# An attention and expert-layer kernel on one Trainium2 core: score buffers, PSUM banks and the turning of tiles redistributed

## The chip, the core and the metric

The kernel runs on one core of a Trainium2 chip. A core has TensorE (PE in the profile; PEld is its loading of weights), VectorE (DVE), ScalarE (ACT), GpSimd (POOL) and SyncE (SP), which here issues all DMAs. They work in parallel, each in its own fixed order, and wait for each other by semaphores. Working memory is SBUF; TensorE writes its results to PSUM, which has eight banks of 512 fp32 columns in each of 128 partitions, and the others read them there. The metric is the time of one execution on the device, in microseconds (us), lower being better.

## The reference

Sparse attention, then two gated feed-forward layers over all tokens:

```
scores = scale * q @ k.T;  thresh = max(scores) - tau          # 4 batches, 8 heads, 576 x 576, head 64
scores = where(scores >= thresh, scores, -1e9)
attn = exp(scores - max(scores));  attn /= sum(attn) + 1e-9
x = attn @ v                                                    # as 2304 tokens x 512
x = x / rms(x) * rms_g
x = (silu(x @ w_gate) * (x @ w_val)) @ w_out                    # 512 -> 1536 -> 512
x = (silu(x @ w_gate2) * (x @ w_val2)) @ w_out2
```

tau is 0.02 here. With a negative one no score of a row would pass, and the reference would give all 576 keys the same weight; the kernel takes care of that case too.

## The kernel before

`body` doesn't issue instructions straight away. Each operation is entered with `op` (L77) in a `Program` with its engine, an estimated cost in ns, the keys that it reads and writes, its buffers and a priority `p` (a due time). `order` (L104) then plays a list schedule with these costs and emits the instructions in the order that it finds. On the chip every engine keeps that order, whatever the true durations are.

**Attention.** A batch has 36 tiles (`NTB`): 4 pairs of heads, 9 tiles of 128 query rows for each pair. `tile_ops` (L368) makes one tile: scores into two PSUM banks (`QK`, L388); the row maximum (L398); from it threshold and bias by `K1`, two constants in spare columns of the score bank (L399); the exponential (L400); the mask, which also sums the row (L401). For the product with the values the masked tile has to be turned. `by_pe` (L206) decides how: on TensorE (five transposes L420, copies out L423, fp32 values L431, output L434), which holds for 24 tiles of batch 0 and 18 of batch 1; or it is split into two fp16 parts (high L441 or L444, low L442 on GpSimd or L445 on VectorE), turned by a DMA transposition (L448), and multiplied with the values in three bf16 parts (L464); one output sums the parts (L469 for two tiles in batches 2 and 3, L472 for one). `finish` (L476) handles a group of nine tiles: rows in which nothing passes get the mean of the values (`v_mean`, L353), and all are scaled by the reciprocal, in six GpSimd operations (L494 to L502). `rms` (L504) normalises a batch and writes it, turned and in two parts, to `XS`, what the dense layers read.

**Dense layers.** Phases in the order of `PHASES` (L186), (batch, layer): (0,0), (1,0), (0,1), (1,1), (2,0), (2,1), (3,0), (3,1). They are called phases 0 to 7 here. A phase has 18 weight units and 36 groups of 12 matmuls (`dense`, L626; matmuls L636), each group in a PSUM bank of its own; the last batch has more columns and two banks for a group. The groups are emptied by L662 and L663 (gate), L666 (value), L691 and L693 (output); L670 and L671 split the hidden part. Weights come as fp64: in phases 0 and 2 each unit is converted (L582 on ScalarE, L585 to L588 on VectorE) and split into two parts (L590, L592: VectorE for the first layer, GpSimd for the second), and kept in device memory for the later phases.

**What sets the order.** `DS` and `DD` (L188) are due times and lengths of the phases, `SPAN` (L199) those of a batch's tiles; `FP` is the planned time of a tile of batch 0. Phase 0 needs all of batch 0, phase 1 all of batch 1, phase 4 batch 2, phase 6 batch 3.

**PSUM.** `SA` (two banks) holds scores; `DA` and `DB` (two each) hold four dense banks, and in batch 0 serve as second score buffer (`DA`) and for transposed tiles (`DB`); two banks `PT` take turns for values and normalisation. From batch 1 on all scores use `SA`, and the fifth transposed piece of a tile goes to its spare columns (L413).

Of the kernel before, what the change touches and what calls it, by code (L numbers as in the profile page):

```python
# [69 lines left out]
class Program:  # L70


    def __init__(self):
        self.eng, self.cost, self.deps, self.fn, self.prio, self.lat, self.name, self.cols, self.rel = [], [], [], [], [], [], [], [], []
        self.wrote, self.read = {}, {}

    def op(self, eng, cost, fn, r=(), w=(), bufs=(), p=0.0, lat=None, name='', cols=None, rel=0.0):  # L77
# [26 lines left out]
    def order(self):  # L104
# [19 lines left out]
        out, seen = [], {}  # L124
        while len(out) < n:
# [46 lines left out]

@with_exitstack
def body(ctx: ExitStack, tc: tile.TileContext, qkv, tau, w1, rg, w2, outT):
# [24 lines left out]
    SPAN = [(A0, A0 + NTB * FP), (DS[0] + 1000, DS[1] - 14000), (DS[1], mid), (mid, DS[6] - 16000)]  # L199
# [21 lines left out]
    ones = sb.tile([P, P], F32, name="ones")  # L221
    nc.gpsimd.memset(ones, 1.0)
# [8 lines left out]
    K1 = SA[:, 0, 508:510]  # L231
# [64 lines left out]
    op("ACT", 200, lambda: nc.scalar.copy(K1, K0), w=["K1"], p=0, name="K1")  # L296
    op("DMA", 625, lambda: nc.sync.dma_start(rgs, rg), w=["rg"], p=9000, name="rg")

    def spread_g():
# [29 lines left out]
    def split_v(hd):  # L329
# [15 lines left out]
        parts = [v.t[:, :, 64 * i:64 * i + 64] for i in range(3)]  # L345
# [3 lines left out]
        for i, x in enumerate((V, R)):  # L349
            op("POOL", 500, lambda i=i, x=x: nc.gpsimd.tensor_scalar(parts[i], x, 1.0, 1.0, ALU.mult, ALU.mult), r=[("rawv", hd)], **k)  # L350
            op("POOL", 800, lambda i=i, x=x: nc.gpsimd.tensor_tensor(R if i == 0 else parts[2], x, parts[i], ALU.subtract), r=[("rawv", hd)], **k)

    def v_mean(g):  # L353

        p = ST(g * NT) + 5 * FP
        pt, pk = next_pt()
        vs = vsum[g]
        vb = r_vb.next()
        op("PE", 400, lambda: nc.tensor.matmul(pt[:, :P], ones, vs.t.rearrange("p h d -> p (h d)"), start=True, stop=True), r=[("vs", 2 * g), ("vs", 2 * g + 1)], w=pk, bufs=[vs], p=p, name=f"vsum{g}")
        for o, i in ((vb.t[:, :P], pt[:, :P]), (vb.t[0:64, P:], pt[0:64, 0:64]), (vb.t[64:, P:], pt[64:, 64:P])):  # L360
            op("ACT", 200, lambda o=o, i=i: nc.scalar.activation(o, i, AF.Copy, scale=UPP), w=pk + [("vb", g)], bufs=[vb], p=p, name=f"vsum{g}")
# [430 lines left out]
```

## Time and profile before

| | |
|---|---|
| Median of 3 runs | 1427.27 us (1425.29 to 1430.33) |
| The profiled execution | 1425.47 us |
| Its span, first to last instruction | 1423.7 us |
| Mean granted TensorE clock | 0.923 of 2.4 GHz |
| PE, DVE, ACT, POOL busy | 1285.2, 781.2, 480.0, 463.0 us |

Times in the rows further down count from the start of the span. A "busy" TensorE is one with a matmul under way; it is not one at its peak. A row of windows gives for one stretch its length, the busy time of each engine with its number of instructions, the mean granted clock (1.00 is 2.4 GHz, 0.50 is 1.2 GHz), the mean busy share of the DMA engines and what they moved. In a group of instructions, "busy" is followed by the mean length of one in ns, then the idle time of its engine just before them and what ended it.

### The profile page before, as it was taken

How to read it: one execution, taken by the hardware profiler on the slowest of the kernel's cores; microseconds unless marked ns; L12 is line 12 of the kernel's file. 1: busy time of each engine (PE TensorE's matmuls, PEld its weight loads, DVE VectorE, ACT ScalarE, POOL GpSimd, SP SyncE). 2: the span in 40 equal slices, each digit the busy share in tenths (PEclk: the TensorE clock that was granted, in tenths of full speed). 3: DMA queues.
4: the chain of work that ended last, by engine and by line, in shares of the span. 5: the costliest groups of instructions: out<-in, count | busy, mean ns of one | idle time of the engine just before them, and what ended most of it. 6: DMA issues, size and time to landing. Idle time of an engine off the chain costs nothing.

```text
span 1423.7 us, 18094 instructions
## 1 busy us (share of the span) xinstructions
PE 1285.2 (90%) x6946; PEld 1024.9 (72%) x6946; DVE 781.2 (55%) x1282; ACT 480.0 (34%) x785; POOL 463.0 (33%) x532
## 2 busy tenths in 40 slices
PE   7988799987659998878899999999999999999998
PEld 5656576664437766655677777677777899999998
DVE  5676699894482448979954655455554311222122
ACT  5653455443341324443333423323332221122110
POOL 5644325252141236563632324132211211132111
PEclk9955699995569999989999999999999999999999
DMA  5366176784255666678796577676666333333332
GB/s 167 85 180 180 42 250 215 249 267 126 58 119 168 191 185 217 203 242 279 226 272 190 176 220 215 182 198 185 185 185 185 130 137 118 121 139 126 119 125 97
DMA packets 178870, 247.47 MB, mean 174 GB/s; under 512 B 141408, under 2 KB 149600, under 8 KB 155744
## 3 DMA queue, kind: packets, MB, share of 16 engines
q1 hardware_dynamic: 178784, 246.32, 56.7%
q8 instruction: 54, 0.88, 0.3%
q14 instruction: 32, 0.26, 0.0%
HBM read 170.40 MB, written 42.47 MB: 150 GB/s over the span
## 4 chain that ended last, share of the span: by engine, by line
PE 72%; DVE 14%; issue 4%; ACT 3%; DMA 3%; POOL 3%; SPq 0%; ACTq 0%; POOLq 0%; DVEq 0%
PE ps L636 57%; PE ps L388 5%; PE pt L464 4%; PE pt L431 3%; DMA U<-U 3%; DVE th L666 2%; DVE col L398 2%; PE ps L420 2%; DVE U L401 1%; DVE U L445 1%; ACT U L400 1%; DVE w L586 1%; DVE Y L693 1%; DVE w L587 1%; DVE w L588 1%
## 5 line engine op out<-in xcount | busy, mean ns | idle before, releaser
L636 PE MATMUL ps<-FU,w 128*128 128x512 f32 (+1 forms) x2592 | 619.3, 391 | 47.2 <-DVE th L666 21.4
L636 PEld LDWEIGHTS ps<-FU,w 128*128 128x128 f32 x2592 | 474.5, 191 | 159.8 <-issue 29.2
L636 PE MATMUL ps<-XS,w 128*128 128x384 f32 (+1 forms) x1728 | 348.4, 359 | 6.0 <-DVE th L666 3.9
L636 PEld LDWEIGHTS ps<-XS,w 128*128 128x128 f32 x1728 | 308.4, 190 | 37.6 <-DVE th L666 10.1
L671 POOL TENSOR_TENSOR FU<-th,FU 128x512 fp32r<-128x512 f32 x72 | 103.7, 1441 | 352.2 <-ACT FU L670 352.2
L400 ACT ACTIVATE U<-ps,col 128x576 f32<-128x576 f32 x144 | 106.5, 741 | 175.1 <-DVE col L399 170.6
L401 DVE SCALAR_TENSOR_TENSOR U<-ps,col,U 128x576 f32<-128x576 f32 x144 | 116.9, 813 | 64.9 <-ACT U L400 64.7
L388 PE MATMUL ps<-U 64*128 64x288 f32 (+1 forms) x640 | 129.4, 527 | 23.4 <-DVE U L401 17.5
L398 DVE TENSOR_REDUCE col<-ps 128x1 f32<-128x576 f32 x144 | 108.3, 752 | 72.4 <-PE ps L388 53.5
L671 POOL TENSOR_TENSOR FU<-U,FU 128x768 fp32r<-128x768 f32 x24 | 44.0, 1834 | 234.8 <-ACT FU L670 234.8
L464 PEld LDWEIGHTS <-U 128*128 128x128 f16 (+1 forms) x1120 | 79.6, 107 | 42.7 <-issue 26.9
L464 PE MATMUL pt<-U,U 128*128 128x192 bf16 (+3 forms) x1120 | 98.4, 249 | 6.6 <-DMA U<-U 6.2
L445 DVE SCALAR_TENSOR_TENSOR U<-U 128x576 f16<-128x576 f32 x90 | 87.5, 972 | 21.3 <-ACT U L444 20.8
L663 DVE SCALAR_TENSOR_TENSOR U<-U,ps 128x768 f32<-128x768 f32 x24 | 22.9, 954 | 134.9 <-ACT U L662 134.9
L388 PEld LDWEIGHTS ps<-U 64*128 64x128 f32 (+1 forms) x640 | 50.9, 204 | 63.8 <-issue 37.7
L666 DVE SCALAR_TENSOR_TENSOR th<-th,ps 128x512 f32<-128x512 f32 x72 | 49.3, 685 | 86.5 <-PE ps L636 86.5
L670 ACT CAST FU<-th 128x512 fp32r<-128x512 f32 x72 | 44.7, 620 | 152.1 <-DVE th L666 152.0
L663 DVE SCALAR_TENSOR_TENSOR th<-th,ps 128x512 f32<-128x512 f32 x72 | 49.2, 683 | 80.3 <-ACT th L662 79.7
L431 PEld LDWEIGHTS pt<-U 128*128 128x128 f32 (+3 forms) x480 | 63.5, 213 | 25.5 <-ACT U L423 8.6
L444 ACT ACTIVATE U<-U 128x576 f16<-128x576 f32 x90 | 61.5, 683 | 54.4 <-DVE U L401 52.4
L431 PE MATMUL pt<-U 128*128 128x64 f32 (+3 forms) x480 | 71.2, 309 | 6.5 <-DVE XB L472 3.7
L662 ACT ACTIVATE th<-ps 128x512 f32<-128x512 f32 x72 | 42.9, 596 | 84.2 <-PE ps L636 82.4
(98 smaller groups left out, 1099.2 us busy)
## 6 DMA issues: line engine op xcount, KB each, us to landing
w<-kept SPq DMA_DIRECT2D x108, 1024.0 KB, 5.0
w<-in_w SPq DMA_DIRECT2D x36, 1024.0 KB, 5.4
kept<-w SPq DMA_DIRECT2D x36, 1024.0 KB, 4.6
U<-in_qkv SPq DMA_DIRECT2D x32, 288.0 KB, 3.5
U<-in_qkv SPq DMA_DIRECT2D x32, 160.0 KB, 3.3
U<-in_qkv SPq DMA_DIRECT2D x64, 72.0 KB, 3.3
out<-Y SPq DMA_DIRECT2D x12, 256.0 KB, 4.0
U<-U SPq DMA_TRANSPOSE x102, 3.4
```

The costliest lines, as they stand in the source:

```text
L388: nc.tensor.matmul(s[m:m + w, j, :HS], x[k, c0:c0 + w], x[k, S:S + HS], start=True, stop=True)
L398: op("DVE", 700, lambda: nc.vector.tensor_reduce(c[:, 0:1], s2, AX.XY, ALU.max, negate=True), w=sk + [("mx", n)], bufs=[cb], p=T + 500, na ...
L400: op("ACT", 690, lambda: nc.scalar.activation(e2, s2, AF.Exp, bias=c[:, 2:3], scale=SCALE), r=[("thr", n)], w=sk + [("e", n)], bufs=[cb, e ...
L401: op("DVE", 850, lambda: nc.vector.scalar_tensor_tensor(e2, s2, c[:, 1:2], e2, ALU.is_ge, ALU.mult, accum_out=sm), r=[("thr", n)], w=sk + ...
L431: nc.tensor.matmul(pt[m:m + w, :D], a[k, i, m:m + w], v[k, i], start=(i == 0), stop=(i == 4))
L444: op("ACT", 620, lambda: nc.scalar.activation(h[:, :S], e, AF.Copy, scale=UPP), r=[("e", n)], w=[("hi", n)], bufs=[eb, hb], p=T + 3000, na ...
L445: op("DVE", 660, lambda: nc.vector.scalar_tensor_tensor(h[:, NE:NE + S], e, UPP, h[:, :S], ALU.mult, ALU.subtract), r=[("e", n), ("hi", n) ...
L464: nc.tensor.matmul(pt[m:m + k, o0:o0 + w], a[:, 5 * j + i, m:m + k], v.t[:, i, :w], start=(j == 0 and i == 0), stop=(j == 1 and i == 4))
L636: nc.tensor.matmul(pt[:, j], wt(i, a), xx[:, j], start=(i == 0 and a == 0 and b_ == 0), stop=(i == 3 and a == 1))
L663: op("DVE", dw, lambda: nc.vector.scalar_tensor_tensor(t2, t2, 1.0, pt, ALU.add, ALU.mult), w=pk + [("th", n)], bufs=[tb], p=T - 6000, nam ...
L666: op("DVE", dw, lambda: nc.vector.scalar_tensor_tensor(t2, t2, 0.5, qt, ALU.mult, ALU.mult), w=qk + [("th", n)], bufs=[tb], p=T - 6000, na ...
L671: op("POOL", pw, lambda: nc.gpsimd.tensor_tensor(h[:, 1], t, f32(h[:, 0]), ALU.subtract), r=[("th", n), ("h0", n)], w=[("h1", n)], bufs=[t ...
```

## The change

- PSUM: two score buffers `SA` and `SB` (batch 0 has `DA` as a third), dense banks `D0`, `D1`, `D2` (two in phase 0, three in phases 1 to 5, in place of four), one bank `PT` for values, which alternates with `D2` in batches 0 and 1. Phases 6 and 7 rotate `SA`, `SB`, `DA`. The threshold's constants stand in each score buffer. The fifth transposed piece of a tile goes to the value banks, not to the score buffer.
- All of batch 0 is turned by DMA; in batch 1 24 of 36 tiles on TensorE (18 before), whose last piece is now 64 rows filled up with zeros by GpSimd. In batch 0 every fourth tile makes its low part on VectorE, the others on GpSimd. Outputs are taken in pairs in batch 0 too.
- The row sums of tiles turned by DMA come from a column of ones beside the values (65 columns for each part); only tiles turned on TensorE still sum in the mask.
- Rows in which nothing passes: four predicated copies on VectorE put the mean there straight from PSUM; GpSimd then has two operations a group in place of six, and ScalarE's three copies go.
- The two casts in the split of the values go from GpSimd to ScalarE; the low part of the second layer's weights (L592) from GpSimd to VectorE.
- The planner gets new costs and due times, and plays operations marked `lock` and all of GpSimd's as excluding each other.

The core of the diff:

```diff
+            if self.lock[i]:
...
+                t = max(t, port)
+                port = t + self.cost[i]
...
-    FP, A0 = 2200, 8000
-    DD = [170000, 125000, 125000, 125000, 120000, 120000, 150000, 150000]
-    DS = [A0 + NTB * FP + 10000]
+    FP, A0 = 2450, 4000
+    DD = [210000, 122000, 126000, 122000, 122000, 120000, 147000, 147000]
+    DS = [A0 + NTB * FP + 40000]
...
-    SPAN = [(A0, A0 + NTB * FP), (DS[0] + 1000, DS[1] - 14000), (DS[1], mid), (mid, DS[6] - 16000)]
+    SPAN = [(A0, A0 + NTB * FP), (DS[0] - 4000, DS[1] - 40000), (DS[1] - 30000, DS[2] - 10000), (DS[3], DS[6] - 60000)]
...
-        return n % 3 != 2 if n < NTB else n < 2 * NTB and n % 2 == 0
+        return NTB <= n < 2 * NTB and n % 3 != 0
...
-    SA, DA, DB = [ps.tile([P, 2, 512], F32, name=f"ps{i}") for i in range(3)]
-    PT = [ps.tile([P, 512], F32, name=f"pt{i}") for i in range(2)]
-    SCORES = [(SA, ["SA"]), (DA, ["D0", "D1"]), (DB, ["D2", "D3"])]
-    BANKS = [(t[:, j], [f"D{2 * i + j}"]) for i, t in enumerate((DA, DB)) for j in range(2)]
+    SA, SB, DA = [ps.tile([P, 2, 512], F32, name=f"ps{i}") for i in range(3)]
+    DC, PT = [ps.tile([P, 512], F32, name=f"pt{i}") for i in range(2)]
+    SCORES = [(SA, ["SA"]), (SB, ["SB"]), (DA, ["D0", "D1"])]
+    BANKS = [(DA[:, 0], ["D0"]), (DA[:, 1], ["D1"]), (DC, ["D2"])]
+    VALUES = [(PT, ["PT"]), (DC, ["D2"])]
...
-    K1 = SA[:, 0, 508:510]
...
+    for t in v5:
+        nc.gpsimd.memset(t[:, :, 0, D:], 1.0)
+        nc.gpsimd.memset(t[:, :, 1:, D:], 0.0)
...
+    def next_bank(first):
+        pti[0] += 1
+        return VALUES[pti[0] % 2] if first else VALUES[0]
...
+        op("ACT", 200, lambda t=t: nc.scalar.copy(t[:, 0, HS:HS + 2], K0), w=k, p=0, name="K1")
...
-            op("POOL", 500, lambda i=i, x=x: nc.gpsimd.tensor_scalar(parts[i], x, 1.0, 1.0, ALU.mult, ALU.mult), r=[("rawv", hd)], **k)
+            op("ACT", 400, lambda i=i, x=x: nc.scalar.copy(parts[i], x), r=[("rawv", hd)], **k)
...
-    def v_mean(g):
...
-        s, sk = SCORES[n % 2] if first else SCORES[0]
+        s, sk = SCORES[n % 3] if first else SCORES[n % 2]
...
+        op("DVE", 180, lambda: nc.vector.scalar_tensor_tensor(c[:, 1:3], s[:, 0, HS:HS + 2], c[:, 0:1], K2, ALU.mult, ALU.add), r=[("mx", n), "tau"] + sk, w=[("thr", n)], bufs=[cb], p=T + 500, name=f"THR{n}")
...
+        op("DVE", 750, lambda: nc.vector.scalar_tensor_tensor(e2, s2, c[:, 1:2], e2, ALU.is_ge, ALU.mult, accum_out=c[:, 3:4] if by_pe(n) else None), r=[("thr", n)], w=sk + [("e", n)], bufs=[cb, eb], p=T + 2000, name=f"MASK{n}")
...
+            op("POOL", 250, lambda: nc.gpsimd.memset(a[64:, 4], 0.0), w=[("az", n)], bufs=[ab], p=T + 1000, name=f"zero{n}")
+            for i0, i1 in ((0, 4), (4, 5)):
+                pt, pk = next_bank(True)
+                f3 = pt.rearrange("p (i q) -> p i q", q=P)[:P if i0 == 0 else 64, :i1 - i0]
...
+                        nc.tensor.transpose(f3[:, i - i0], e[:, i * P:min(S, (i + 1) * P)], ident)
...
+                op("PE", 110 * (i1 - i0), turn, r=[("e", n)], w=pk, bufs=[eb], p=T + 4000, name=f"TE{n}")
+                op("ACT", 120 + 110 * (i1 - i0), lambda f3=f3, i0=i0, i1=i1: nc.scalar.copy(a[:f3.shape[0], i0:i1], f3), w=pk + [("at", n)], bufs=[ab], p=T + 3500, name=f"TEout{n}")
...
-            if first:
+            if first and n % 4 != 3:
...
-            pairs = b > 1
+            paired = b != 1
...
+                pvb[0] = next_bank(b < 2)
...
-                    w = (192, 128)[j]
+                    w = (3 - j) * E
...
+                            nc.tensor.matmul(pt[m:m + k, :w], a[:, 5 * j + i, m:m + k], v[:, i, :w], start=(j == 0 and i == 0), stop=(j == 1 and i == 4))
...
-        vb = v_mean(g)
...
+        op("DVE", 100, lambda: nc.vector.tensor_scalar(q[:, 0], s, 0.0, None, ALU.is_equal), r=xk, **k)
+        op("DVE", 100, lambda: nc.vector.scalar_tensor_tensor(q[:, 1], q[:, 0], float(S) * UPP, s, ALU.mult, ALU.add), r=xk, **k)
+        op("DVE", 100, lambda: nc.vector.tensor_scalar(q[:, 2], q[:, 1], 1e-9 * UPP, None, ALU.add), **k)
+        op("DVE", 100, lambda: nc.vector.reciprocal(q[:, 3], q[:, 2]), **k)
...
+        pt, pk = next_bank(g < 2 * NP)
...
+        op("PE", 400, lambda: nc.tensor.matmul(pt[:, :P], ones.to_broadcast([P, P]), vs.t.rearrange("p h d -> p (h d)"), start=True, stop=True), r=[("vs", 2 * g), ("vs", 2 * g + 1)], w=pk, bufs=[vs], p=T - 1000, name=f"vsum{g}")
+        none = q[:, 0].bitcast(U32)
+        for h in range(2):
+            m = slice(64 * h, 64 * h + 64)
+            d = pt[:, 64 * h:64 * h + 64]
+            op("DVE", 350, lambda h=h, d=d: nc.vector.copy_predicated(X[:, h:8:2, :D], none[:, h:8:2].unsqueeze(2).to_broadcast([P, 4, D]), d.unsqueeze(1).to_broadcast([P, 4, D])),
+               r=[("rec", g)], w=pk + xk[h:8:2], bufs=[sb_, xb], p=T - 1000, name=f"fall{g}")
+            op("DVE", 150, lambda m=m, d=d: nc.vector.copy_predicated(X[m, 8, :D], none[m, 8:9].to_broadcast([64, D]), d[m]),
+               r=[("rec", g)], w=pk + xk[8:9], bufs=[sb_, xb], p=T - 1000, name=f"fall{g}")
...
+        op("POOL", 1250, lambda: nc.gpsimd.tensor_tensor(O[:, :8], X8, q[:, 3, :8].unsqueeze(2).to_broadcast([P, 8, D]), ALU.mult), r=[("rec", g)] + xk[:8], w=[("XB", gp, i) for i in range(8)], p=T, **kk)
+        op("POOL", 290, lambda: nc.gpsimd.tensor_tensor(O[:, 8], x8, q[:, 3, 8:9].to_broadcast([P, D]), ALU.mult), r=[("rec", g)] + xk[8:9], w=[("XB", gp, 8)], p=T + 100, **kk)
...
-        p = T - 9000
+        p = T - 13000
...
+        p = T - 10000
...
-        e, c, n1 = ("POOL", 2300, nc.gpsimd) if m else ("DVE", 1135, nc.vector)
-        op(e, c, lambda: n1.tensor_tensor(ws[:, 1], w, f32(ws[:, 0]), ALU.subtract), r=[("w32", n), ("wh", n)], w=[("wl", n)], bufs=[b32, sbf], p=p, name=f"w_split{n}")
+        op("DVE", 1135, lambda: nc.vector.tensor_tensor(ws[:, 1], w, f32(ws[:, 0]), ALU.subtract), lock=True, r=[("w32", n), ("wh", n)], w=[("wl", n)], bufs=[b32, sbf], p=p, name=f"w_split{n}")
...
-            pt, pk = BANKS[turn3[0] % 4]
+            pt, pk = BANKS[turn3[0] % (3 if k else 2)]
```

## Rows read from the trace of the kernel before

**Rows 1.** Busy time by stage: length, PE, PEld, DVE, ACT, POOL, clock, DMA share, GB/s
```profile
7.00:80.00 73.00, 63.84 (x437) 45.51 (x436) 49.48 (x114) 43.40 (x80) 47.20 (x83) 0.89 0.47 123
165.00:322.00 157.00, 146.79 (x809) 112.35 (x808) 134.75 (x197) 77.10 (x126) 60.94 (x59) 0.97 0.70 232
322.00:420.00 98.00, 59.95 (x310) 40.48 (x309) 58.05 (x119) 35.69 (x72) 29.45 (x49) 0.58 0.35 86
548.00:713.00 165.00, 136.21 (x645) 99.30 (x640) 149.55 (x183) 70.55 (x97) 93.95 (x64) 0.93 0.73 238
713.00:1117.00 404.00, 386.58 (x2074) 286.92 (x2072) 213.26 (x391) 127.53 (x220) 108.92 (x138) 1.00 0.69 200
```

**Rows 2.** Timeline (start, us, engine, line): batch 0's last maximum, first dense matmuls
```profile
128.58 0.76 DVE L398 TENSOR_REDUCE col<-ps 128x1 f32<-128x576 f32 x1
...
162.27 4.93 PE L636 MATMUL ps<-FU,w 128*128 128x512 f32 x12
```

**Rows 3.** The same windows for L398, one maximum for each tile
```profile
7.00:80.00 73.00, 17.98 (x25) 0.89 0.47 123
...
322.00:420.00 98.00, 12.80 (x17) 0.58 0.35 86
548.00:713.00 165.00, 11.19 (x15) 0.93 0.73 238
```

**Rows 4.** Timeline of one tile between 355 and 362.5 us, waits in brackets
```profile
355.10 1.33 PE L388 MATMUL ps<-U 64*128 64x288 f32 x4
...
356.78 0.76 DVE L398 TENSOR_REDUCE col<-ps 128x1 f32<-128x576 f32 x1 [2.20 <-ACT U L423]
...
359.48 1.33 PE L388 MATMUL ps<-U 64*128 64x288 f32 x4 [0.53 <-DVE U L401]
```

**Rows 5.** Timeline of TensorE between 40 and 60 us, at the full clock
```profile
51.35 0.77 PE L420 MATMUL ps<-ident,U 128*128 128x128 f32 x5
51.95 0.85 PE L464 MATMUL pt<-U,U 128*128 128x192 bf16 x10
...
55.58 0.76 PE L388 MATMUL ps<-U 64*128 64x288 f32 x4
57.00 1.47 PE L431 MATMUL pt<-U 128*128 128x64 f32 x10 [0.66 <-ACT U L423]
```

**Rows 6.** Timeline of TensorE between 129 and 141 us, at half clock
```profile
132.08 1.54 PE L464 MATMUL pt<-U,U 128*128 128x192 bf16 x10
```

**Rows 7.** Groups of instructions by form: busy, mean ns of one, idle before, releasers
```profile
L401 DVE SCALAR_TENSOR_TENSOR U<-ps,col,U 128x576 f32<-128x576 f32 x144 | 116.9, 813 | 64.9 <-ACT U L400 64.7
...
L398 DVE TENSOR_REDUCE col<-ps 128x1 f32<-128x576 f32 x144 | 108.3, 752 | 72.4 <-PE ps L388 53.5 <-ACT U L423 18.2
...
L445 DVE SCALAR_TENSOR_TENSOR U<-U 128x576 f16<-128x576 f32 x90 | 87.5, 972 | 21.3 <-ACT U L444 20.8
...
L586 DVE TENSOR_SCALAR w<-w 128x1024 uint32<-128x1024 uint32 x36 | 47.0, 1305 | 0.3
...
L399 DVE SCALAR_TENSOR_TENSOR col<-ps,col,K 128x2 f32<-128x2 f32 x144 | 30.7, 215 | 10.3 <-PE ps L388 7.5 <-ACT U L400 0.2
...
L469 DVE TENSOR_REDUCE XB<-pt 128x128 f32<-128x384 f32 x32 | 17.7, 552 | 1.6 <-PE pt L464 1.5
```

**Rows 8.** Line L448, the DMA transposition: least, median and longest issue in ns
```profile
L448 SPq DMA_TRANSPOSE U<-U x102: 1259/1347/2853, 20.1 to 1094.4; - x102
```

**Rows 9.** TensorE's timeline at 715 us; the dense group by form
```profile
715.36 3.02 PE L636 MATMUL ps<-FU,w 128*128 128x512 f32 x12
...
L636 PE MATMUL ps<-FU,w 128*128 128x512 f32 x2016 | 518.5, 407 | 47.2 <-DVE th L666 21.4 <-POOL w L592 6.5 <-DVE Y L693 5.5
```

**Rows 10.** Lines L586 and L592 one by one: least, median and longest ns
```profile
L586 DVE TENSOR_SCALAR w<-w x36: 676/854/2924, 70.2 to 700.2; 128x1024 uint32<-128x1024 uint32 x36
...
L592 DVE TENSOR_TENSOR w<-w,w x18: 1208/1219/2316, 81.7 to 313.3; 128x1024 fp32r<-128x1024 f32 x18
L592 POOL TENSOR_TENSOR w<-w,w x18: 2357/2396/3315, 535.9 to 708.2; 128x1024 fp32r<-128x1024 f32 x18
```

More of the change, by code (lines that the diff above doesn't have):

```diff
@@ L123, in order @@
                 arrive(i)
-        out, seen = [], {}
+        out, seen, port = [], {}, 0.0
         while len(out) < n:
@@ L276, in body @@
     XB = sb.tile([P, NP, 9, D], F32, name="XB")
-    SM = [sb.tile([P, NP, 9], F32, name=f"SM{i}") for i in range(2)]
+    r_x = ring("x", 2, [P, 9, E], F32)
     r_v2 = ring("v2", 1, [P, 5, D], F32)
-    r_col = ring("col", 6, [P, 3], F32)
+    r_col = ring("col", 6, [P, 4], F32)
     r_sm = ring("sm", 2, [P, 4, 9], F32)
     r_vs = ring("vs", 2, [P, 2, D], F32)
-    r_vb = ring("vb", 2, [P, 3 * D], F32)
-    r_tmp = ring("tmp", 1, [P, 8, D], F32)
     r_xn = ring("xn", 2, [P, NC, P], F32)
@@ L344, in split_v @@
         op("POOL", 290, lambda: nc.gpsimd.tensor_tensor(o[0:64], o[0:64], V[0:64, 4], ALU.add), **k)
-        parts = [v.t[:, :, 64 * i:64 * i + 64] for i in range(3)]
+        parts = [v.t[:, :, i, :D] for i in range(3)]
         rb = r_v2.next()
@@ L349, in split_v @@
         for i, x in enumerate((V, R)):
-            op("POOL", 500, lambda i=i, x=x: nc.gpsimd.tensor_scalar(parts[i], x, 1.0, 1.0, ALU.mult, ALU.mult), r=[("rawv", hd)], **k)
+            op("ACT", 400, lambda i=i, x=x: nc.scalar.copy(parts[i], x), r=[("rawv", hd)], **k)
             op("POOL", 800, lambda i=i, x=x: nc.gpsimd.tensor_tensor(R if i == 0 else parts[2], x, parts[i], ALU.subtract), r=[("rawv", hd)], **k)
-    def v_mean(g):
[L355 to L361, printed above, removed]
-        return vb
     SLOT = [0, 2, 4, 6, 8, 1, 3, 5, 7]
-    pvb = {}
+    pvb, xr = {}, {}
     def tile_ops(n):
@@ L448, in tile_ops @@
             op("DMA", 1500, lambda: nc.sync.dma_start_transpose(out=a, in_=h), r=[("hi", n), ("lo", n)], w=[("at", n)], bufs=[hb, ab], p=T - 8000, name=f"DT{n}")
-            pairs = b > 1
-            second = pairs and t in (1, 3, 6, 8)
+            paired = b != 1
+            second = paired and t in (1, 3, 6, 8)
             if not second:
-                pvb[0] = next_pt()
-            pt, pk = pvb[0]
-            o0 = 192 if second else 0
-            vs = [vv[hd] for hd, *_ in rows]
+                pvb[0] = next_bank(b < 2)
@@ L459, in PV @@
+            pt_, pk = pvb[0]
+            pt = pt_[:, 256 * second:]
+            vs = [vv[hd].t.rearrange("p c k d -> p c (k d)") for hd, *_ in rows]
             def PV():
                 for j in range(2):
-                    w = (192, 128)[j]
+                    w = (3 - j) * E
                     for i in range(5):
                         for v, (_, _, k, m) in zip(vs, rows):
-                            nc.tensor.matmul(pt[m:m + k, o0:o0 + w], a[:, 5 * j + i, m:m + k], v.t[:, i, :w], start=(j == 0 and i == 0), stop=(j == 1 and i == 4))
```

141 lines of the change are left out of this document (56 added, 85 removed).

## The prediction

> **What bounds the kernel now.** I first read busy times between the first and last records of each stage [rows 1]. In 7 to 80 us (most of batch 0) TensorE is busy 63.84 of 73 us. The rest of batch 0 (last maximum at 129), its normalisation and the first weight conversions fill the time to the first dense matmul at 162 [rows 2]. From 165 to 322 phase 0 keeps TensorE (146.79 of 157) and VectorE (134.75) nearly full. From 322 to 420 no dense work is left, because phase 1 needs all of batch 1: TensorE is busy 59.95 of 98 us at a granted clock of 0.58, VectorE 58.05, so nothing is full. From 420 TensorE is the bound (386.58 of 404 in 713 to 1117), except in 548 to 713, where the second matrix set is converted and VectorE is busy 149.55 of 165. What follows 1117 is the last two phases, whose operations the change leaves as they are.
>
> The counts of tiles by stage are in [rows 3]: 25 in the first 73 us, 17 in 322 to 420. The timeline of one tile there [rows 4] shows why it is so slow: scores (1.33 us) start at 355.10, and VectorE's maximum starts at 356.78, released by ScalarE's L423, which copies a transposed piece out of the spare columns of the same score buffer. Threshold, exponential and mask follow one by one, and the next scores start at 359.48, released by the mask (L401). One score buffer makes a serial loop of 4.4 us a tile, 5.8 with what else the stage waits for (98/17).
>
> **What a tile costs.** At the full clock (2.4 GHz) TensorE takes 0.76 us for scores, 0.77 for five transposes, 1.47 for the values of a tile turned on TensorE and 0.85 for those of a tile turned by DMA [rows 5]. So the first kind costs 3.00 us, the second 1.61. At half clock the DMA kind costs 1.33 + 1.54 = 2.87 [rows 4, 6]. On VectorE each tile has a maximum 0.752, threshold 0.215, mask 0.813; the fp16 low part, where VectorE makes it, 0.972; the output of a pair 0.552 [rows 7].
>
> **Batch 0.** Now 24 of 36 tiles are turned on TensorE: 2/3 x 3.00 + 1/3 x 1.61 = 2.54 us a tile against a pace of 73/25 = 2.92, so TensorE bounds it and is 87% full. The change turns all by DMA and rotates three score buffers. Then VectorE leads: 0.752 + 0.215 + 0.813 + 0.972/4 + 0.552/2 = 2.30. At the same 87% the pace is 2.64; 36 tiles take 95 us from 7 on, to 102 (now 129). From the last maximum to the first dense matmul 33 us pass now; that chain (mask, parts, transposition, values, scaling, normalisation) stays. On GpSimd it loses two of three large operations, on VectorE it gains predicated copies; I take that as even. Conversions that stand between the tiles cost some 3 us more than the gap covers. First dense matmul: 102 + 33 + 3 = 138. **Term 1: -24.**
>
> SP's queue: 24 more transpositions, each 1.347 us of issue [rows 8], are 32 us more on SP during batch 0; all 36 take 49 of 95 us, beside the loads. Behind a transposition that waits for its low part stand the loads of the next heads, and the scores wait for those. I cost it at nothing because SP stays near two thirds full; without that cover the price is up to the 32 us. The six fewer transpositions of batch 1 take 8 us off SP where it isn't the bound. On GpSimd the two casts of each head go to ScalarE, which was busy well under its span [rows 1].
>
> **Phase 0 with batch 1.** Now 258 us (162 to 420). TensorE: 36 dense groups of 12 matmuls at 3.02 us [rows 9] are 109; 36 tiles with 24 on TensorE, 2.54 each, 91; sums and normalisation 3: 203. VectorE: a weight unit is two one-input conversions, 0.68 and 0.85 (least and median of L586), and three two-input ones like L592's 1.22 [rows 10], together 5.2; 15 are left: 78. Dense evacuations, 32 at about 0.69 (a mask of 576 columns takes 0.813, these have 512): 22. Tiles, 36 at 0.752 + 0.215 + 0.813 + (0.972 + 0.4)/3 + 0.05 = 2.29: 82. Predicated copies and reciprocals 12, normalisation 8: 202. Both engines are near 202. The second score buffer and the move of the transposed pieces to the value banks open the loop of [rows 4]. At TensorE's 93% of [rows 1] (146.79/157) the stage takes 217; the tail goes, and what is late next is VectorE. **Term 2: 217 - 258 = -41.** Bounds: 202 with nothing lost (-56), and 258 if the tail stays (0).
>
> Predicated copies appear in no row. Nearest are the output sums that VectorE reads from PSUM, 0.552 [rows 7]; a quarter of that, about 0.2, is the lower end for one of four copies, a mask's 0.813 the upper; a gain is excluded, since they are added. Four a group: 0.8 to 3.3 us, over 16 groups 13 to 52. I take 0.45 each, 29 us. In 713 to 1117 VectorE has 190 us to spare [rows 1], so the 8 groups of batches 0 and 1 count, 14 us, of which 7 lie in the 202 above and 7 in batch 0's loss. The ones column widens the value matmuls from 192 to 195 columns (1.6% of 0.85) and drops the mask's accumulator read: nothing.
>
> **Phases 1 to 5.** Now 697 us. In 548 to 713 the low part of 18 weight units moves from GpSimd (median 2.396) to VectorE (1.219) [rows 10]: +22 us on VectorE where it is nearly full. Against it, conversion L586 takes 1.305 us on average [rows 7] but 0.676 at least [rows 10], the spread of an operation that is held up. 0.63 us less on each of two such conversions in 18 units gives back up to 23. [...] VectorE's load there stays equal. Batch 2 is wanted before phase 2, which takes tiles out of it (15 now, [rows 3]); each costs VectorE near 3 us there, and TensorE 1.61 in phase 1. 8 tiles x 1.4 = 11. **Term 3: -12**, bounds -35 (all 15 and the freed spread) and +20 (VectorE's 22 with nothing freed).
>
> Two or three dense banks in place of four: a group fills a bank in 3.02 us [rows 9], VectorE empties it in 0.69. With two banks a release may come 2.3 us late before TensorE waits, with three 5.3. That slack covers it, so nothing; without it, see the last rival but one. One value bank in batches 2 and 3: two values of 0.85 and an output of 0.552 in two tiles' time of 404/36 = 11.2 us each: covered. **Term 4: 0.**
>
> **Sum.** 1425.47 (the profiled execution, 1.8 under the median of the runs, 1427.27) - 24 - 41 - 12 = 1348.
>
> **Rivals.**
> *Better, 1305.* VectorE runs without gaps in batch 0 (36 x 2.30 = 83, first dense matmul at 123, -39), phase 0 takes 202 (-56), phases 1 to 5 lose 25. For it: three score buffers and a bank for each use. Against it: no stage before 1117 keeps its bound engine over 96% [rows 1]. Chance 0.16.
>
> *The clock stays low, 1385.* TensorE has 1.61 us of work in a pace of 2.64 in batch 0. In 322 to 420, busy 61% of the time, it was granted 0.58; in 7 to 80, busy 87%, 0.89 [rows 1]. If batch 0 runs at half clock, TensorE bounds it: 2.87/0.87 = 3.3 a tile, 119 us, first dense matmul at 159 (-3). With all of term 2 that gives 1369, with half 1390: about 1385. [...] Against it: at half clock 2.87 us would fill the pace. Chance 0.18.
>
> *Slower, 1456.* Its place is the dense evacuation. With fewer banks a release that VectorE makes late stops TensorE, and conversions of 1.2 us stand in VectorE's fixed order. Of the waits before these matmuls, 47.2 us in all, 21.4 end with L666 even with four banks [rows 9]. If each of 216 groups in phases 0 to 5 waits 0.5 us more, the price is 108: 1348 + 108. It decides from 77/216 = 0.36 us a group on. Against it: the slack of 2.3 and 5.3 us. Chance 0.12.
>
> *No change, 1425.* The planned order does what it did, batch 1 still trails phase 0, and VectorE's added 22 + 14 us eat terms 1 and 3. Chance 0.04.
>
> The forecast has 0.50.
>
> **Numbers.** A measurement of this kernel can tell about 0.3% (4 us) from no change. Faster: 0.50 + 0.16 + 0.18 = 0.84, less 0.01 for a low clock that costs still more: 0.83. Same 0.05, slower 0.12. The range, 1295 to 1405, takes in the better rival and the low clock with the unknown costs, and leaves out the slower one, no change and a little below.
>
> **What would show it.** Right: first dense matmul near 138; batch 0 at some 2.6 us a tile; no long stretch without dense matmuls before phase 1, which starts near 355; scores no longer released by the mask; phase 2 no longer than 165; the last two phases as now. Wrong: a granted clock near 0.5 through batch 0 (the second rival); waits before dense matmuls far over 47 us with VectorE as releaser (the third); a gap before phase 1 as long as now (the fourth).

## The result, and the profile after

The changed kernel takes 1364.2 us (median of 4 runs, 1363.41 to 1367.02) against 1427.2 for the kernel before in the same comparison: a ratio of 0.956, 95% interval 0.954 to 0.958. The profiled execution took 1363.4 us, with a span of 1361.6 and a mean granted clock of 0.962.

Where the 62 us of span went, by stages that begin with the first dense matmul of a phase (read from each trace's dense matmuls, 12 to a group, 36 groups to a phase). "Apart" is the same kernel with one line changed, explained below.

| us | before | after | predicted | before, apart | after, apart |
|---|---|---|---|---|---|
| first dense matmul | 162.3 | 143.6 | 138 | 163.4 | 143.3 |
| phase 0 with batch 1 | 256.3 | 217.9 | 217 | 250.4 | 217.5 |
| phases 1 to 5 | 698.2 | 695.8 | 685 | 667.1 | 647.3 |
| phases 6 and 7, end | 306.9 | 304.3 | as now | 306.7 | 304.3 |
| span | 1423.7 | 1361.6 | | 1387.7 | 1312.5 |

The windows of the kernel after, by stage, columns as in [rows 1]:

```profile
7.00:80.00 73.00, 48.13 (x372) 30.95 (x369) 56.83 (x115) 51.51 (x89) 48.55 (x70) 0.84 0.97 200
144.00:361.00 217.00, 196.02 (x1152) 143.49 (x1151) 178.11 (x311) 117.86 (x238) 71.94 (x97) 0.96 0.66 213
...
361.00:528.00 167.00, 158.85 (x979) 114.03 (x978) 123.22 (x217) 72.17 (x115) 43.84 (x59) 0.98 0.81 203
528.00:670.00 142.00, 118.72 (x496) 87.34 (x495) 128.85 (x163) 65.09 (x91) 31.72 (x29) 0.96 0.77 262
670.00:1057.00 387.00, 363.06 (x1881) 274.52 (x1882) 166.56 (x283) 103.22 (x170) 69.94 (x77) 1.00 0.61 182
```

And the maxima in the same windows (L400 now), one for each tile, as in [rows 3]:

```profile
7.00:80.00 73.00, 20.72 (x28) 0.84 0.97 200
144.00:361.00 217.00, 26.79 (x36) 0.96 0.66 213
...
361.00:528.00 167.00, 23.32 (x31) 0.98 0.81 203
528.00:670.00 142.00, 5.22 (x7) 0.96 0.77 262
670.00:1057.00 387.00, 21.94 (x29) 1.00 0.61 182
```

Two rows of the kernel before for the same line, its phase 1 and its phases 3 to 5:

```profile
420.00:548.00 128.00, 7.56 (x10) 0.99 0.62 182
713.00:1117.00 404.00, 32.48 (x43) 1.00 0.69 200
```

The first row of the stages: TensorE fell from 63.84 to 48.13 us busy in batch 0 and the DMA engines rose from 0.47 to 0.97; 28 tiles lie in it where 25 did. The timeline gives the stage's two ends, as in [rows 2]:

```profile
105.45 0.75 DVE L400 TENSOR_REDUCE col<-ps 128x1 f32<-128x576 f32 x1
...
143.60 5.54 PE L634 MATMUL ps<-FU,w 128*128 128x512 f32 x12
```

The stretch of 98 us without dense work ahead of phase 1 is now 10 us (last dense matmul of phase 0 at 351, phase 1 at 361). Tiles moved forward: 31 lie in phase 1 in place of 10, 7 in phase 2 in place of 15, 29 in phases 3 to 5 in place of 43. Yet phases 1 to 5 together are only 2.4 us shorter. That is where the expected gain is missing. Waits of the kernel after in batch 0 (from 7 to 106 us; total, times, longest), and the dense groups by line and tile:

```profile
PEld L462 <- DMA U<-U: 29.1, 16, 3.8
PE pt L462 <- DMA U<-U: 22.1, 12, 3.4
...
DVE col L400 <- PE ps L391: 14.2, 6, 7.0
...
DVE x L467 <- PE pt L462: 12.2, 8, 3.9
```

```profile
L634 PE MATMUL ps<-FU,w 128*128 128x512 f32 (+1 forms) x2040 | 484.1, 386 | 42.7 <-DVE th L661 15.0 <-ACT th L660 7.0 <-DVE Y L691 6.2
L634 PE MATMUL ps<-XS,w 128*128 128x384 f32 (+1 forms) x1560 | 308.4, 353 | 11.4 <-DVE th L661 8.6 <-DVE th L664 1.0 <-DVE Y L691 0.8
...
L634 PE MATMUL pt<-FU,w 128*128 128x512 f32 x552 | 142.3, 402 | 4.7 <-DVE w L590 4.7
L634 PE MATMUL pt<-XS,w 128*128 128x512 f32 x168 | 42.7, 398 | 0.0
```

`ps` is the two-bank tile `DA` (and, in phases 6 and 7, the score buffers), `pt` the single bank `DC`. Groups in `DA` wait for VectorE and ScalarE; groups in `DC` wait only for converted weights. That row was the lead for the most telling experiment.

### The profile page after: what moved, and what is told of

Its sections match the earlier page's. It is cut to its first block, busy times and chain, and to the rows that moved or that the text cites. A ratio compares the mean times of both kernels' runs of the same rounds, so it can differ in the third digit from the quotient of the medians.

```text
span 1361.6 us, 17956 instructions
## 1 busy us (share of the span) xinstructions
PE 1223.1 (90%) x6856; PEld 975.8 (72%) x6856; DVE 769.7 (57%) x1249; ACT 497.9 (37%) x830; POOL 349.2 (26%) x433
## 4 chain that ended last, share of the span: by engine, by line
PE 71%; DVE 14%; DMA 8%; issue 3%; ACT 3%; POOL 1%; SPq 0%; DVEq 0%; ACTq 0%; POOLq 0%
PE ps L634 49%; PE pt L634 10%; DMA U<-U 6%; PE pt L462 5%; PE ps L391 4%; DVE th L661 2%; DVE U L403 2%; PE pt L428 1%; DVE w L590 1%; DVE w L586 1%; DVE w L587 1%; ACT th L660 1%; DVE col L400 1%; DVE U L443 1%; DVE th L664 1%
## 5 line engine op out<-in xcount | busy, mean ns | idle before, releaser
L634 PE MATMUL ps<-FU,w 128*128 128x512 f32 (+1 forms) x2040 | 484.1, 386 | 42.7 <-DVE th L661 15.0
L634 PEld LDWEIGHTS ps<-FU,w 128*128 128x128 f32 x2040 | 368.7, 190 | 129.9 <-DVE th L661 24.9
L634 PE MATMUL ps<-XS,w 128*128 128x384 f32 (+1 forms) x1560 | 308.4, 353 | 11.4 <-DVE th L661 8.6
L634 PEld LDWEIGHTS ps<-XS,w 128*128 128x128 f32 x1560 | 274.0, 188 | 35.9 <-DVE th L661 12.0
L634 PE MATMUL pt<-FU,w 128*128 128x512 f32 x552 | 142.3, 402 | 4.7 <-DVE w L590 4.7
L462 PEld LDWEIGHTS <-U 128*128 128x128 f16 (+1 forms) x1320 | 94.7, 106 | 71.9 <-DMA U<-U 45.6
L462 PE MATMUL pt<-U,U 128*128 128x195 bf16 (+3 forms) x1320 | 115.2, 249 | 33.2 <-DMA U<-U 30.9
L400 DVE TENSOR_REDUCE col<-ps 128x1 f32<-128x576 f32 x144 | 107.5, 752 | 52.3 <-PE ps L391 51.6
L634 PEld LDWEIGHTS pt<-FU,w 128*128 128x128 f32 x552 | 102.7, 191 | 31.1 <-DVE w L590 5.5
L661 DVE SCALAR_TENSOR_TENSOR th<-th,ps 128x512 f32<-128x512 f32 x57 | 39.1, 686 | 105.6 <-ACT th L660 54.0
L661 DVE SCALAR_TENSOR_TENSOR U<-U,ps 128x768 f32<-128x768 f32 x24 | 22.9, 955 | 132.3 <-ACT U L660 132.3
L660 ACT ACTIVATE th<-ps 128x512 f32<-128x512 f32 x57 | 34.0, 596 | 85.3 <-PE ps L634 80.8
L660 ACT ACTIVATE U<-ps 128x768 f32<-128x768 f32 x24 | 19.5, 813 | 106.4 <-PE ps L634 106.4
```

What stands on the lines that cost most here:

```text
L400: op("DVE", 750, lambda: nc.vector.tensor_reduce(c[:, 0:1], s2, AX.XY, ALU.max, negate=True), w=sk + [("mx", n)], bufs=[cb], p=T + 500, na ...
L462: nc.tensor.matmul(pt[m:m + k, :w], a[:, 5 * j + i, m:m + k], v[:, i, :w], start=(j == 0 and i == 0), stop=(j == 1 and i == 4))
L634: nc.tensor.matmul(pt[:, j], wt(i, a), xx[:, j], start=(i == 0 and a == 0 and b_ == 0), stop=(i == 3 and a == 1))
L660: op("ACT", aw, lambda: nc.scalar.activation(t2, pt, AF.Tanh, scale=0.5), w=pk + [("th", n)], bufs=[tb], p=T - 6000, name=f"tanh{n}")
L661: op("DVE", dw, lambda: nc.vector.scalar_tensor_tensor(t2, t2, 1.0, pt, ALU.add, ALU.mult), w=pk + [("th", n)], bufs=[tb], p=T - 6000, nam ...
```

## The experiments

Each was run once beside the kernel before, but for the last, which was timed in rounds. Runs of the kernel before lay between 1419 and 1432 us. Three theories stood at the start: the second score buffer gives the gain (Buffers), the due times give it (Due times), or the planner's truer costs and its lock (`port` in the diff) do (Costs).

**One score buffer.**

```diff
-        s, sk = SCORES[n % 3] if first else SCORES[n % 2]
+        s, sk = SCORES[n % 3] if first else SCORES[0]
```

> The changed kernel with a single score buffer from batch 1 on (SB stays unused until phases 6 and 7). Three theories of where the 63 us came from. Buffers: the second score buffer opens the serial loop of a tile in phase 0 and phase 1; without it the stretch from the first dense matmul of phase 0 to that of phase 1, 218 us, goes back to 245 or more, phase 1 gets longer, and the time is 1390 to 1415. Due times: the new phase lengths and spans alone remove the tail; the time stays under 1375. Costs: the plan played with truer costs and the port lock does it; under 1375 as well.

Measured 1409.7 us. Phase 0's stage takes 262.0 us, as long as before, and all other parts of the change are still in it. Its last 78 us show the tail of [rows 1] again, low clock included; the last 47 of them, the second row, are without dense matmuls, where the kernel after has 10:

```profile
322.00:400.00 78.00, 55.21 (x284) 37.78 (x281) 47.99 (x96) 33.16 (x73) 22.85 (x38) 0.70 0.41 122
353.00:400.00 47.00, 29.22 (x161) 18.95 (x160) 29.28 (x61) 21.70 (x49) 10.82 (x20) 0.64 0.35 84
```

The second score buffer carries term 2: undoing it alone gives the stage back 44 us. Phase 1, which was expected to get longer, got 14 us shorter, and phase 2 got 20 longer.

**Due times.** First the kernel after with the old ones, then the kernel before with the new ones (`FP`, `A0`, `DD`, `DS`, `SPAN` exchanged as in the diff).

> The changed kernel with the due times of before (FP, A0, DD, DS, SPAN), all else kept. Due times: batch 1 trails phase 0 again, a stretch of 50 us or more without dense matmuls comes back ahead of phase 1, 1400 or more. Buffers, costs: the tail stays short, 1360 to 1380.

> The kernel of before with the due times of the changed one alone. Due times: most of the gain is there, 1375 to 1395. Buffers, costs: within 10 us of 1427, since a single score buffer keeps the loop of 4.4 us a tile.

Measured 1380.9 and 1418.9 us, both as Buffers and Costs had it, the first 0.9 above their range. In the kernel after the old times cost 17 us, 8 of them before the first dense matmul (151.7), and no tail comes back (stage 223.4); 2.5 more lie in the last two phases. In the kernel before the new times alone bring the first dense matmul to 141.6 and the last maximum of batch 0 to 106.2, without any tile turned otherwise; but the stage of phase 0 stays at 256.3. Its windows, and behind them one of the kernel before:

```profile
7.00:80.00 73.00, 64.41 (x473) 45.79 (x469) 48.11 (x118) 44.16 (x84) 45.50 (x82) 0.93 0.46 119
80.00:106.00 26.00, 23.28 (x180) 16.99 (x180) 18.39 (x45) 16.48 (x32) 15.30 (x26) 0.93 0.40 92
```

```profile
80.00:106.00 26.00, 22.03 (x107) 14.98 (x105) 19.60 (x42) 15.23 (x26) 9.42 (x15) 0.57 0.73 215
```

With the conversions no longer put between the tiles (the first begins at 103.9 us here, at 66.5 in the kernel before), TensorE issues 180 matmuls in 26 us at a granted clock of 0.93, where it issued 107 at 0.57. Up to the first dense matmul the due times alone are worth as much as the whole of term 1. Two of the five weight units that the kernel before converts ahead of that matmul come behind it here. Not all of it is a gain: phases 1 to 5 grow from 698.2 to 715.0, with 26 tiles in phase 1 in place of 10, and the whole is 4 us shorter than the kernel before on the same chip (1422.6), which one run hardly tells from nothing.

**Old costs, no lock.** The kernel after, its order planned with the costs of the kernel before and without the exclusion, for instance

```diff
-            self.lock.append(lock or eng == 'POOL')
+            self.lock.append(False)
...
-                op("PE", int(227 * fw) * len(part), emit, r=wkeys + [k for i in used for k in xkeys(i)], w=pk, bufs=bufs, p=T + U * c0 / len(mms), name=name)
+                op("PE", int(216 * fw) * len(part), emit, r=wkeys + [k for i in used for k in xkeys(i)], w=pk, bufs=bufs, p=T + U * c0 / len(mms), name=name)
```

> The changed kernel planned with the costs of before and without the lock between VectorE and GpSimd; what is computed, the banks and the due times are the changed kernel's. Costs: engines wait for each other in an order that doesn't fit their true durations, 1390 or more, with TensorE's waits for VectorE longer in phases 0 to 2. Buffers, due times: 1360 to 1372.

Measured 1358.5 us, 6 below the kernel after and 1.5 below the range of Buffers and Due times. The Costs theory falls.

**Batch 0 turned on TensorE again.**

```diff
-        return NTB <= n < 2 * NTB and n % 3 != 0
+        return n % 3 != 2 if n < NTB else n < 2 * NTB and n % 3 != 0
...
-            paired = b != 1
+            paired = b > 1
```

> The changed kernel with 24 of batch 0's 36 tiles turned on TensorE again (outputs of batch 0 one by one). Turning theory (the prediction's first term): TensorE then bounds batch 0 at 2.9 us a tile, the first dense matmul comes at 152 or later and the time is 1372 or more. Due-time theory (the kernel of before with the new due times alone had its first dense matmul at 141.6): the first dense matmul stays at 139 to 147, the time within 6 us of 1364.

Measured 1369.8 us. The two theories share the result: the first dense matmul comes at 159.4, 16 later, as the turning theory has it, but the stage of phase 0 shrinks from 217.9 to 204.2, and the time is within 6 us, as the due-time theory has it. Part of the 16 is work that only changed sides: five weight units are converted ahead of the first dense matmul here, three in the kernel after. The last maximum of batch 0 comes at 113.8, 8 later. Turning batch 0 by DMA is worth about 6 us in all, not the 24 that stand beside it in term 1.

**The low part of the second layer's weights on GpSimd again** (the two removed lines of `w_split` put back).

> The changed kernel with the low part of the second layer's weights on GpSimd again (18 operations). Load theory: 18 x 1.3 us come off VectorE in phase 2, which is 8 us or more shorter than 142; 1350 to 1357. Port theory: GpSimd's 2.4 us operations hold VectorE's conversions, phase 2 is 8 us or more longer; 1371 to 1385. Both cancel, as the prediction's third term put it: within 6 us.

Measured 1368.5 us; phase 2 takes 146.6 in place of 142.1. VectorE's busy time in it hardly falls. By group, from 527 to 674 us of this run (phase 2 begins at 529.6) and in phase 2 of the kernel after:

```profile
L586 DVE SCALAR_TENSOR_TENSOR w<-w,w 128x1024 uint32<-128x1024 uint32 x15 | 25.7, 1715 | 0.0
L587 DVE SCALAR_TENSOR_TENSOR w<-w,w 128x1024 uint32<-128x1024 uint32 x16 | 24.3, 1521 | 0.0
```

```profile
L586 DVE SCALAR_TENSOR_TENSOR w<-w,w 128x1024 uint32<-128x1024 uint32 x16 | 21.6, 1352 | 0.0
L587 DVE SCALAR_TENSOR_TENSOR w<-w,w 128x1024 uint32<-128x1024 uint32 x16 | 21.2, 1328 | 0.0
```

With GpSimd at work on 2.6 us operations, VectorE's conversions grow by 0.36 and 0.19 us here and by 0.23 and 0.11 in the two one-input ones: 0.9 us a unit, 13 for the 15 units in this stretch. That takes back most of the 20 that VectorE is spared there (16 operations of 1.26). TensorE waits a little longer for the low parts: 12.2 us of its idle time end with GpSimd's L591, where 8.0 ended with VectorE's L590. The time is within 6 us, as the third theory had it.

**Predicated copies left out.** This kernel doesn't do what the reference asks for rows in which nothing passes (with this tau there are none).

```diff
-        for h in range(2):
...
-            op("DVE", 350, lambda h=h, d=d: nc.vector.copy_predicated(X[:, h:8:2, :D], none[:, h:8:2].unsqueeze(2).to_broadcast([P, 4, D]), d.unsqueeze(1).to_broadcast([P, 4, D])),
...
-            op("DVE", 150, lambda m=m, d=d: nc.vector.copy_predicated(X[m, 8, :D], none[m, 8:9].to_broadcast([64, D]), d[m]),
```

> The changed kernel without the four predicated copies of each group (left out: the means for rows in which nothing passes, of which this data has none). As the prediction put it, only the 8 groups of batches 0 and 1 lie on the path, 1.34 us each by the trace of the changed kernel: 5 to 12 us less, 1352 to 1359. Rival, all 16 groups are beside the path: within 4 us of 1364.

Measured 1345.2 us, 19 less, outside both ranges. The copies themselves, line by line in the kernel after (least, median, longest ns):

```profile
L496 DVE COPY_PREDICATED x<-sm,pt x32: 395/446/460, 43.0 to 1004.4; 128x256 f32<-128x256 uint32 x32
```

```profile
L498 DVE COPY_PREDICATED x<-sm,pt x32: 201/224/240, 46.5 to 1004.9; 64x64 f32<-64x64 uint32 x32
```

A group takes 2 x 0.446 + 2 x 0.224 = 1.34 us, the 8 groups of batches 0 and 1 take 10.7. The first dense matmul comes 6.9 us earlier, phase 0's stage is 9.5 shorter. The 8 us beyond the copies' own time asked for a reason. One candidate was the bank: the ones-column product writes a value bank that stays taken until the last copy, 11 to 15 us later in these groups.

```diff
-r=[("vs", 2 * g), ("vs", 2 * g + 1)], w=pk, bufs=[vs]
+r=[("vs", 2 * g), ("vs", 2 * g + 1), ("rec", g)], w=pk, bufs=[vs]
```

> The kernel after, with the ones-column product of a group issued only behind its reciprocals, so that it holds a value bank until the copies for a shorter time than the 11 to 15 us of the kernel after; the copies themselves stay. Holding theory (what the copies cost beyond their own 10.7 us is the bank that they keep from the weighted sums): batch 0 and the stage of phase 0 get shorter by 1 to 2 us a group of heads, 1348 to 1358 us. Rival (it is VectorE's queue: the copies stand ahead of maxima): within 4 us of 1364.

Measured 1366.1 us. In batches 0 and 1 the bank is now held for 3 to 10 us. The stage of phase 0 is 6 us shorter, as the holding theory had it, but the first dense matmul is 4.7 later and phase 1 2.6 longer; the span is 2 above that of the kernel after. So a shorter holding gained nothing in all, and the number is the rival's; that VectorE's queue is the cause is not shown by it. What the other 8 us are stays open.

**Neighbouring dense groups in different tiles.** `DA` is one tile of two banks, `D0` and `D1`. Consecutive groups take banks in turn, so in phases 1 to 5 one pair of neighbours in three lies in the two halves of `DA`.

```diff
-            pt, pk = BANKS[turn3[0] % (3 if k else 2)]
+            pt, pk = BANKS[(0, 2, 1, 2)[turn3[0] % 4] if k else turn3[0] % 2]
```

> The changed kernel with the dense banks of phases 1 to 5 taken in the order D0, D2, D1, D2 in place of D0, D1, D2, so that two groups in a row never lie in the two halves of one tile. Tile theory: the seventh matmul of a group waits for the readers of the group before, because both banks belong to one tile; these waits (15 to 20 us in phases 1 to 5) go and the time is 1345 to 1356. Bank theory: what counts is that three banks are too few; D2 is now filled again after two groups, waits grow, 1368 or more. Neither: within 4 us of 1364.

Measured 1314.3 us, 50 less than the kernel after, and 31 less than the lower end of what the tile theory expected. Phases 1 to 5 lose 7.1, 11.0, 10.4, 8.7 and 11.2 us. Phases 3 to 5 in a row of windows, to be set beside the last one of the kernel after above:

```profile
652.00:1008.00 356.00, 354.37 (x1882) 275.13 (x1881) 165.38 (x283) 103.05 (x170) 70.06 (x77) 1.00 0.65 199
```

Nearly the same number of matmuls, 1882 and 1881, fills 354.37 of 356 us, where 363.06 of 387 were busy. How the loss came about stands in the timeline of the kernel after. At 808.47 begin the last six matmuls of a gate and, without a gap, the first six of its value group, both in `ps`:

```profile
808.47 3.00 PE L634 MATMUL ps<-FU,w 128*128 128x512 f32 x12
...
811.56 0.60 ACT L660 ACTIVATE th<-ps 128x512 f32<-128x512 f32 x1 [2.84 <-PE ps L634]
812.26 0.69 DVE L661 SCALAR_TENSOR_TENSOR th<-th,ps 128x512 f32<-128x512 f32 x1 [2.35 <-ACT th L660]
813.00 1.66 PE L634 MATMUL ps<-FU,w 128*128 128x512 f32 x6 [1.54 <-DVE th L661]
```

The gate is complete at 810, but its reader, the tanh, starts at 811.56, behind the six matmuls that write the other half. Then the other half's next six matmuls wait until the gate's readers are done, 1.54 us. Neither touches the other's bank. These are the waits that accesses tracked by tile, in the order of issue, would give: six matmuls of the neighbour, the readers, six matmuls of the neighbour. Of the 36 gates in phases 3 to 5, 10 have a tanh that starts 1.46 to 1.48 us behind the last matmul of its group, just six matmuls of 0.24; in the run with the banks apart none does, and most start 0.10 behind. There the same place reads:

```profile
772.51 1.52 PE L634 MATMUL ps<-FU,w 128*128 128x512 f32 x6
...
772.77 0.60 ACT L660 ACTIVATE th<-pt 128x512 f32<-128x512 f32 x1 [2.57 <-PE pt L634]
773.48 0.69 DVE L661 SCALAR_TENSOR_TENSOR th<-th,pt 128x512 f32<-128x512 f32 x1 [2.56 <-ACT th L660]
774.65 1.65 PE L634 MATMUL ps<-FU,w 128*128 128x512 f32 x6
```

The 15 to 20 us of waits that the tile theory started from were too few. TensorE's waits for readers of dense groups in `ps`, in phases 1 to 5 of the kernel after:

```profile
PE ps L634 <- DVE th L661: 18.5, 18, 1.5
PE ps L634 <- ACT th L660: 6.5, 6, 1.8
PE ps L634 <- DVE Y L691: 5.5, 6, 1.6
...
PE ps L634 <- DVE th L664: 3.6, 6, 0.9
```

They come to 34 us, and 5 such are left with the banks apart. That is 29 of the 48; the rest is not broken down by any run.

**The same in the kernel before**, whose four banks are the halves of two tiles.

```diff
-            pt, pk = BANKS[turn3[0] % 4]
+            pt, pk = BANKS[(0, 2, 1, 3)[turn3[0] % 4]]
```

> The kernel before, with its four dense banks taken in the order 0, 2, 1, 3, so that two consecutive groups never lie in the two halves of one tile; nothing else. Tile theory: half of the neighbours shared a tile in the kernel before as well, so its phases 1 to 5 (131, 166, 134, 133 and 135 us) lose some 5 to 10 us each and the kernel comes to 1375 to 1400 us. Rival (four banks already covered it, and the 50 us belong to the three banks of the change): 1418 to 1428 us, every phase within 3 us of the kernel before.

Measured 1389.5 us, 42 below the kernel before on the same chip and 36 below its profiled execution. Phases 1 to 5 lose 10.2, 6.4, 6.4, 3.0 and 5.1 us, 31 together, phase 0 5.9. The dense groups in phases 1 to 5, first of the kernel before, then of this run:

```profile
L636 PE MATMUL ps<-FU,w 128*128 128x512 f32 x1584 | 405.3, 406 | 37.1 <-DVE th L666 16.6 <-POOL w L592 6.5 <-DVE Y L693 4.5
```

```profile
L636 PE MATMUL ps<-FU,w 128*128 128x512 f32 x1584 | 400.3, 404 | 15.0 <-POOL w L592 9.0 <-DVE th L663 4.7 <-ACT th L662 1.2
```

No wait of dense matmuls for L666 is left in these phases. So it never was a late release of a group's own bank.

**Phase 0 too.** The three banks in that order in phase 0 as well; the values of batch 1 then have one bank, not two.

```diff
-            pt, pk = BANKS[turn3[0] % (3 if k else 2)]
+            pt, pk = BANKS[(0, 2, 1, 2)[turn3[0] % 4]]
...
-                pvb[0] = next_bank(b < 2)
+                pvb[0] = next_bank(b < 1)
```

> As the run with the banks of phases 1 to 5 apart (1314 us), with phase 0 taking the same order of three banks, and the values of batch 1 therefore in one bank instead of two. Tile theory: the stage of phase 0 and batch 1 (217 us there) loses about 10 us as the other phases did, 1298 to 1310 us. Rival (batch 1 needs its second value bank more than the dense groups need their tile): that stage becomes longer, 1320 to 1345 us.

Measured 1342.1 us, the rival's number. The dense groups of phase 0 do end 9 us sooner (341.3 for 350.4), but batch 1 falls behind: 44 us pass from there to phase 1 at 385.3, where 10 did. With the values in one bank, the tail is back; the run changes the dense banks of phase 0 along with them, so the two aren't told apart.

**The best two together**: banks apart in phases 1 to 5, and the old costs without the lock.

> The two versions that were faster than the kernel after, in one: phases 1 to 5 with neighbouring dense groups in different tiles (1314 us), and the order planned with the costs of the kernel before, without the lock (1358 us, 6 below the kernel after). If the two gains lie in different places, 1305 to 1311 us. Rival (what the older costs gave was fewer waits on the shared tile, which are gone with the banks apart): 1312 to 1318 us.

Measured 1315.8 us (median of 4 runs, 1313.3 to 1318.2), ratio to the kernel before 0.922, interval 0.918 to 0.926. The number is the rival's, but its reason isn't. What the old costs gave lay in the stage of phase 0 (213.5 us for 217.9), whose banks are taken in the same order in all these runs, and most of it is still there: 214.1 where the run with the banks apart has 217.5. What is new is a loss: phases 1 to 5 take 654.6 us in place of 647.3. With the order of banks changed, the interval ends well below the 0.954 at which that of the change begins.

## Why the prediction was right, and where its steps failed

The forecast, 1348, lies 15 us below the 1363.4 of the profiled execution. By its terms: 5 from term 1, 3 from term 2, 10 from term 3, and 2.6 the other way from the last two phases, which were put as unchanged (304.3 for 306.9). Those 2.6 are the due times: 304.2 in the kernel before with the new ones, 306.8 in the kernel after with the old ones. But for these, the errors of the terms all go the same way and don't cancel, so luck doesn't lie in the sum; it lies in term 1.

**Term 1, batch 0 (-24 put, -18.7 measured): size near, in part by luck, cause misplaced.** "36 tiles take 95 us from 7 on": they took 98.5, 2.7 us a tile. But the step "Then VectorE leads", with the same 87% full, failed: from 7 to 106 us VectorE waits 26 us for TensorE's scores and weighted sums, and TensorE waits for transpositions, with the DMA engines at 0.97 up to 80. (The 2.30 us a tile are lengths added up. Added up so, VectorE's are 64 of 73 us, the 87% put; but they overlap, and the row has 56.83, 78%.) SP's queue was costed "at nothing": a transposition now lands 3.9 us after its issue (median, 3.4 before), and its longest issue is 4.2 us, where it was 2.9 [rows 8]. And the gain isn't the turning's alone. In the kernel before, the due times alone bring the first dense matmul forward by 20.7; in the kernel after, undoing them costs 8 there and 17 in all, and turning batch 0 on TensorE again 16 there and 6 in all. The two don't add up, and part of each is weight units that change sides. I read the busy share of TensorE up to 80 us, and missed that from 80 to 129, where conversions stand between the tiles, its granted clock is 0.57. That the clock stays low, the second rival, came true in part: 0.84 over the first 73 us against 0.89, with TensorE a quarter less busy; over all of batch 0 it is 0.80 against 0.76.

**Term 2, phase 0 (-41 put, -38.4 measured): right**, by the mechanism named. One buffer gives all of it back. The loads were near too: VectorE's lengths add up to 199 us where 202 was put, and TensorE is busy 196.02 where 203 was. Taking the second value bank away from batch 1 gives half of it back, in a run that changes phase 0's dense banks as well.

**Term 3, phases 1 to 5 (-12 put, -2.4 measured): the term that was mis-sized, in the main because term 4 was.** In the kernels as they are, the shared tile takes 31.1 us of these phases before and 48.5 after. With neighbours apart in both, they fall from 667.1 to 647.3, by 20; 17 of the 20 are given back in the shared tile. What the 20 are made of no run tells. The step named for them, tiles taken forward, isn't shown to pay: in the kernel after with the old due times the tiles stay where they were (8, 14 and 43 in phase 1, in phase 2 and in phases 3 to 5), and phases 1 to 5 take 696.8, only 1.0 more. There, 23 more tiles in phase 1 cost 36.5 us, 1.6 each as put, but 7 fewer in phase 2 give back 14.6, 2.1 each where near 3 was put. That the weights' low part would nearly cancel was right (+22 against -23 was put, and putting it back changes phase 2 by 4.5), its price was not: the freed time is 13 us, spread over four conversions, where 23 on two was put. The 23 was an estimate from the spread of L586 alone, and no run shows that all of it goes with the operations that leave GpSimd: with the low parts there again, VectorE's conversions in phase 2 grew by 0.9 us a unit, of which the same conversion has 0.11. The lower bound of the term, -35, doesn't come out of what it names: 15 tiles at 1.4 and the freed spread are -22.

**Term 4, dense banks (0 put): wrong, and the "slower" rival saw the right rows with the wrong mechanism.** Both argued with the number of banks and how soon VectorE empties one. The 21.4 us of waits for L666 in [rows 9] were in front of me "even with four banks"; the slack is 5.3 us with three banks and one more group's 3.02 with four, and couldn't explain them, and that contradiction should have been followed. The waited-for group was not the last user of the bank but the neighbour in the tile. Before the change the first of such a pair is always a value or output group, with one reader; after, it is one pair in three of any kind, with gate and value among them, and a gate has two readers in a row, the tanh and a product. So fewer shared pairs cost more. The last is argued from the order and the releasers (L660 and L661 in place of L666), not tried by itself.

**Predicated copies (0.45 each put):** 0.446 and 0.224 measured, 1.34 us a group where 1.8 was put; but taking them away gives 19 us, more than the 14 that counted. Holding the bank for less gained nothing in all; what the excess is stays open.

## What to carry to other kernels

Where an instruction waits for a reader that it has no data in common with, look at what the two share as a tile: here two halves of one two-bank tile were treated as one, and an order of banks in which neighbours lie in different tiles was worth some 36 to 42 us before the change and 50 after it, with no operation more or less. A wait that remains although the slack worked out should cover it is a lead, not a remainder. Before a gain is put to an engine's load, look at what the plan's due times move into the stretch: undo the times alone first, and look at the whole time as well: a mark such as the first dense matmul moves with what the order puts in front of it.

## What was not expected of the hardware

From 80 to 106 us the granted clock was 0.93 with the new due times and 0.57 without, with nearly the same busy time (23.28 and 22.03 of 26 us) and the same kinds of work on TensorE, 180 and 107 matmuls. Four weight units converted before 106 us, where the run with the new times has one, went with a clock that was lower by 0.36. COPY_PREDICATED with PSUM as source took 446 ns for 256 elements in each of 128 partitions and 224 for 64 in 64, and VectorE's one-input conversion of 1024 elements had a mean of 852 ns, where [rows 7] has 1305. Where the second layer's weights are converted, 15 of these operations had a mean of 1910 in the kernel before (548 to 713 us), 961 in the kernel after (528 to 670) and 1071 with the low parts back on GpSimd (527 to 674), so most of that drop isn't due to the 2.4 us operations leaving GpSimd, the move against which term 3 set it.
